# Squares of batch 0's values summed on the tensor engine, the cast of x moved to GpSimd, and a new place table

## The chip, the cores and the metric

The kernel runs on one core of a Trainium2 chip. The metric is device time in microseconds (us) of one execution: 903.31 us is the median of three runs before the change (902.73 to 905.12). The core has five engines that run side by side, each working through its own list of instructions in order: PE (matmuls), DVE (vector), ACT (activations), POOL (GpSimd) and SP, which here issues every DMA.

## The reference, cut to what matters

Attention over 4 batches, 8 heads, 768 positions and 64 dimensions. Each query and key is assigned to the nearest of 16 centroids, and a score counts only between positions of the same cluster. The result is the input of a feed-forward layer with a mish-like gate.

```python
q_assign = np.argmax(np.einsum('bhsd,hcd->bhsc', q_n, c_n), axis=-1)
k_assign = np.argmax(np.einsum('bhsd,hcd->bhsc', k_n, c_n), axis=-1)
mask = q_assign[:, :, :, None] == k_assign[:, :, None, :]
scores = np.where(mask, scale * np.matmul(q, k.transpose(0, 1, 3, 2)), -1e9)
attn = softmax(scores)
x = np.matmul(attn, v)                 # to (3072 tokens, 512)
h = x @ w_in                           # (3072, 2048)
sp = log1p(exp(h))
out = (h * np.tanh(sp)) @ w_out        # (3072, 512)
```

## The kernel before, in words

**The work.** A unit is one head of one batch and 256 query rows; there are 96 units, and each has two halves of 128 rows. For a half, PE makes a 128x768 tile of scores (`scores`, L611 and L616; the cluster mask is part of that matmul), DVE takes the row maximum (`rowmax`, L626), and ACT takes the exponential with its row sum (`expo`, L640). The two score tiles that can exist at once are the buffers of tag `S` in PSUM: a third score waits until an exponential has freed one. In the first 24 units (batch 0) the probabilities stay f32: PE transposes them (`turn`, L701), ACT copies them back (`back_t`, L717), and PE multiplies them with the raw f32 values (`pv`, L748). Later units split them into two f16 parts (L684 on ACT, L695 on DVE), which a DMA transposes, and use values that are scaled and split as well. `pv_scale` and `pv_out` put the result into a tile `xf` of 128x256; `x_out` (L817) casts it to f16 on ACT and `x_low` (L825) subtracts that on POOL to get the low part. The feed-forward part multiplies these two f16 parts with two f16 parts of the weights: `m1` (L845 to L847, three products each), mish on ACT, a high part on POOL (`e_gh`, L859) and a low part on DVE (`e_gl`, L867), and `m2` (L883 to L885).

**The scales.** The splits need a common scale for the weights and one for each batch of values. For the weights, `w_sq` lets PE multiply bf16 copies of each weight tile with themselves into a PSUM tile `gram`, whose diagonal is then the sum of squares; `w_sum` takes the diagonal and adds it up on DVE. For the values, `v_sq` (L351) squares each of a batch's four tiles on ACT and reads out a row sum; `v_sum` takes the largest of the four sums, and `v_turn`, `v_top`, `v_all` and `v_scale` spread one number over all partitions. Of batch 0 that number scales `pv_scale`'s copy of the row sums (L786).

**The head.** In the first 75 us or so all weights come in as 64-bit floats, by 32 DMAs of 512 KB, and are turned into f32 by ACT (`w_abs`, L264) and DVE (`w_f32`, L272, and `w_or`, L279). Their staging buffers are few, so a DMA can wait on SP, and hold up those behind it, until `w_or` has freed one. `warm` puts 24 groups of 8 matmuls of 128 columns on PE that only add to an unused corner of `gram` (L291).

**The order.** It is written out: `PLAN` gives each operation a place, and the program issues operations in the order of their places (`Plan.run`). An operation calls first what it depends on. So each engine's list follows from that table, and an engine that stands at an instruction whose input is late waits, with all behind it.

Of the kernel before, what the change touches and what calls it, by code (L numbers as in the profile page):

```python
# [56 lines left out]
def tile_clustered_attention_mish_ffn(  # L57
# [175 lines left out]
    wss = cp.tile([P, 32], F32, name="wss")  # L233
    nc.vector.memset(wss, 0.0)
# [58 lines left out]
    def w_sq(n):  # L293


        pl.after(("w_or", n), ("warm", 0), *((("w_sq", n - 1),) if n % 16 else ()))
        i, hf = divmod(n, 2)
        f = W[i + 1][:, hf * 512 : (hf + 1) * 512]
        if n == 16:
            pl.after(*(("warm", k) for k in range(T["warm"])))  # L300
            st["gram", 1] = ps.tile([P, 512], F32, tag="O", name=f"gram{n}", bufs=T["O"])
        o = st["gram", n // 16][:, :P]
        x = f.bitcast(BF16).rearrange("p (c n t) -> p c n t", c=4, t=2)[:, :, :, 1]
        for c in range(4):
            nc.tensor.matmul(
                o, x[:, c], x[:, c], start=(c == 0 and n % 16 == 0), stop=(c == 3 and n % 16 == 15),
                skip_group_check=True,
            )

    def w_sum(part):  # L310

        pl.after(*(("w_sq", part * 16 + n) for n in range(16)))
        n = part * 16 + 15
        junk = gp.tile([P, P], F32, tag="g", name=f"wq{n}")
        nc.vector.tensor_tensor(junk, st["gram", part][:, :P], ident, op=ALU.mult)
        nc.vector.tensor_reduce(wss[:, n : n + 1], junk, axis=AX.X, op=ALU.add)
        norm_sum(wss[:, part * 16 : part * 16 + 16], f"ws{part}", cp, f"ws{part}")
# [492 lines left out]
    def x_out(i):  # L810
# [143 lines left out]
def places(args, text):  # L954
# [4 lines left out]
    'w_load': places(spread(range(0, 32)), """  # L959
        19 25 0 32 24 26 21 89 30 83 87 91 157 189 220 251 84 86 45 43 151 132 207 305 253 293 326 329 370 371 397 428  # L960
    """),
    'centroids': places([()], """
        1
    """),
    'cent_norm': places([()], """
        2
    """),
    'cent_log': places([()], """
        3
    """),  # L970
# [3 lines left out]
    'qk_load': places(spread(range(0, 32)), """  # L974
        12 23 88 90 346 405 659 520 813 745 981 1049 1160 1273 1490 1362 1731 1732 1884 1784 2050 2087 2185 2367 2525
        2422 2597 2720 2835 2979 3008 3140
    """),
    'prep_sc': places(spread(range(0, 32)), """
        13 55 173 197 478 589 741 760 932 913 986 1251 1332 1428 1559 1431 1771 1870 2013 2066 2128 2284 2287 2479 2587
        2654 2659 2892 3005 3102 3185 3269  # L980
    """),
    'prep_hi': places(spread(range(0, 32)), """
        14 56 200 342 479 590 742 806 933 1025 1148 1252 1333 1429 1560 1662 1772 1871 2014 2067 2176 2285 2389 2480
        2588 2655 2787 2893 3006 3103 3186 3293
    """),
    'copy_t': places(spread(range(0, 32)), """
        15 58 201 364 480 593 765 823 946 1047 1149 1257 1355 1436 1582 1665 1778 1901 2041 2082 2192 2289 2429 2497
        2590 2738 2788 2896 3007 3104 3187 3296
    """),
    'w_abs': places(spread(range(0, 32)), """  # L990
        20 73 68 69 31 82 33 183 117 120 164 211 214 229 272 300 141 142 161 162 230 231 265 347 328 334 377 378 395 396
        440 477
    """),
    'cent_root': places([()], """
        22
    """),
    'cent_turn': places([()], """
        27
    """),
    'cent_put': places([()], """  # L1000
        28
    """),
    'assign_mm': places(spread((0, 1)), """
        29 54
    """),
    'prep_lo': places(spread(range(0, 32)), """
        41 57 241 373 500 591 743 839 944 1045 1154 1253 1354 1434 1581 1663 1773 1872 2015 2069 2178 2286 2411 2481
        2589 2656 2796 2894 3031 3116 3240 3294
    """),
    'copy_a': places(spread(range(0, 32)), """  # L1010
        42 59 286 415 539 618 772 930 987 1052 1155 1293 1356 1516 1583 1667 1826 1936 2042 2139 2193 2340 2448 2502
        2591 2761 2797 2945 3056 3174 3247 3344
    """),
    'v_load': places(spread(range(0, 4), range(0, 4)), """
        44 74 81 62 252 530 206 687 1109 1137 1530 1501 1907 1980 2225 2463
    """),
    'w_f32': places(spread(range(0, 32)), """
        46 98 101 104 60 108 138 194 118 121 165 238 267 266 273 301 152 148 222 280 254 262 310 365 339 343 400 408 436
        454 441 503
    """),  # L1020
    'w_or': places(spread(range(0, 32)), """
        47 99 102 105 61 109 158 257 119 122 166 239 268 270 274 327 153 149 223 281 255 271 311 366 340 344 401 409 437
        455 442 504
    """),
    'copy_z': places(spread(range(0, 32)), """
        48 77 242 374 501 592 744 840 945 1046 1176 1263 1388 1435 1604 1664 1777 1900 2048 2081 2201 2288 2412 2496
        2652 2737 2857 2895 3032 3117 3241 3295
    """),
    'assign_hot': places(spread((0, 1)), """
        49 70  # L1030
    """),
    'assign_first': places(spread((0, 1)), """
        50 71
    """),
    'assign_put': places(spread((0, 1)), """
        51 78
    """),
    'rows_z': places(spread((0, 1)), """
        52 79
    """),  # L1040
    'rows_t': places(spread((0, 1)), """
        53 80
    """),
    'hot_copy': places(spread(range(0, 32)), """
        63 187 318 473 580 594 766 842 947 1126 1177 1264 1389 1437 1605 1666 1779 1902 2072 2083 2270 2290 2430 2498
        2653 2739 2871 2897 3074 3118 3242 3297
    """),
    'copy_b': places(spread(range(0, 32)), """
        64 163 269 416 552 635 812 841 988 1048 1247 1267 1456 1526 1668 1753 1816 1932 2049 2107 2217 2300 2446 2562
        2683 2751 2858 2929 3033 3123 3249 3326  # L1050
    """),
    'scores': places(spread(range(0, 96), (0, 1)), """
# [9 lines left out]
    """),  # L1062
    'rowmax': places(spread(range(0, 96), (0, 1)), """
# [9 lines left out]
    """),  # L1073
    'expo': places(spread(range(0, 96), (0, 1)), """
# [261 lines left out]
```

## Time and profile before

| what | value |
|---|---|
| median of three runs | 903.31 us (902.73 to 905.12) |
| profiled execution | 905.48 us |
| its span, first to last instruction | 903.7 us |
| mean granted clock of PE in it | 0.985 of full speed |
| PE, ACT, DVE, POOL busy | 95%, 75%, 68%, 24% |

The profiled execution is 1.8 us longer than its span. The views show, for each engine, when it was busy and what ended each of its waits. A wait is put down to what came last. Busy PE is not always useful PE: `warm` counts as busy, and so does a matmul at half clock.

### The profile page before, as it was taken

Reading aid. Unit: us, or ns where it says so; the run is one execution under the profiler, and the core shown is the slowest. Engines: PE = TensorE matmul, PEld = TensorE weight load, DVE = VectorE, ACT = ScalarE, POOL = GpSimd, SP = SyncE. Lnnn points to the kernel's source line nnn. Section 1 sums busy time; section 2 is a strip of 40 time slices with the busy share of each in tenths; the row PEclk is TensorE's granted clock in tenths of the full one; section 3 lists DMA queues with packets and bytes.
Section 4 is the critical chain, followed back from the end, with each engine's and each line's share of the span. In section 5 each row is a group of like instructions: output and inputs, shape, how many; then the busy total and the mean of one; then the engine's idle time right before and its main releaser. Section 6 shows DMA issues by size and latency. Waiting matters only on the chain. (4 is left out here: it accounts for less than half of the span.)

```text
span 903.7 us, 16486 instructions
## 1 busy us (share of the span) xinstructions
PE 858.8 (95%) x6247; PEld 614.0 (68%) x6247; DVE 613.9 (68%) x1081; ACT 677.9 (75%) x1114; POOL 214.0 (24%) x323
## 2 busy tenths in 40 slices
PE   6788998999999999999999999999999999999997
PEld 6666776768676576586766765677666675776583
DVE  7897887887766777976866778776678766412020
ACT  4777787799899798899998988888889986421020
POOL 2110653432122322312212212132321311112020
PEclk9898999899999999999999999999999999999999
DMA  9787432275666675876957678865659667300000
GB/s 327 262 229 219 106 91 67 53 168 108 127 144 147 128 144 128 181 159 138 155 114 152 133 144 156 154 143 102 129 119 177 120 128 142 72 17 1 24 13 23
DMA packets 252398, 116.19 MB, mean 129 GB/s; under 512 B 230624, under 2 KB 232544, under 8 KB 252320
## 3 DMA queue, kind: packets, MB, share of 16 engines
q1 hardware_dynamic: 252320, 115.15, 57.6%
q8 instruction: 49, 0.80, 0.4%
q14 instruction: 29, 0.24, 0.1%
HBM read 35.68 MB, written 6.29 MB: 46 GB/s over the span
## 5 line engine op out<-in xcount | busy, mean ns | idle before, releaser
L845 PE MATMUL h<-x,w 128*128 128x256 f16 x768 | 209.9, 273 | 1.9 <-ACT u L855 1.9
L847 PE MATMUL h<-x,w 128*128 128x256 f16 x768 | 209.3, 273 | 0.0
L846 PE MATMUL h<-x,w 128*128 128x256 f16 x768 | 209.3, 273 | 0.0
L640 ACT ACTIVATE p<-s,m 128x768 f32<-128x768 f32 x192 | 172.7, 900 | 33.8 <-DVE m L626 18.9
L626 DVE TENSOR_REDUCE m<-s 128x1 f32<-128x768 f32 x192 | 180.8, 949 | 24.7 <-PE s L616 23.6
L695 DVE SCALAR_TENSOR_TENSOR hl<-p,l,hl 128x768 f16<-128x768 f32 x142 | 145.1, 1029 | 47.8 <-ACT hl L684 43.5
L883 PE MATMUL O<-w,g 128*128 128x512 f16 x384 | 146.1, 381 | 1.6 <-ACT osb L891 1.6
L884 PE MATMUL O<-w,g 128*128 128x512 f16 x384 | 145.5, 379 | 0.0
L885 PE MATMUL O<-w,g 128*128 128x512 f16 x384 | 145.5, 379 | 0.0
L684 ACT ACTIVATE hl<-p,l 128x768 f16<-128x768 f32 x142 | 130.1, 929 | 19.2 <-ACT p L640 7.7
L611 PE MATMUL s<-A,B 128*128 128x384 f32 x384 | 120.6, 396 | 24.1 <-ACT p L640 16.6
L867 DVE SCALAR_TENSOR_TENSOR g<-u,mscg,g 128x512 f16<-128x512 f32 x96 | 74.9, 793 | 98.7 <-POOL g L859 98.5
L859 POOL TENSOR_SCALAR g<-u,mscg 128x512 f16<-128x512 f32 x96 | 70.2, 736 | 221.2 <-ACT u L855 200.5
L855 ACT ACTIVATE u<-h,msch 128x512 f32<-128x512 f32 x96 | 63.7, 685 | 69.0 <-PE h L847 50.6
L616 PE MATMUL s<-Z,T 80*128 80x384 f32 x384 | 101.9, 347 | 3.1 <-DMA T<-stg 3.1
L92 ACT ACT_TABLE_LOAD x78 | 100.1, 1283 | 2.1 <-PEq L1326 0.7
L611 PEld LDWEIGHTS s<-A,B 128*128 128x128 f32 x384 | 63.3, 193 | 50.4 <-ACT p L640 30.2
L845 PEld LDWEIGHTS <-w 128*128 128x128 f16 x768 | 75.1, 98 | 21.1 <-issue 10.2
L846 PEld LDWEIGHTS <-w 128*128 128x128 f16 x768 | 75.3, 98 | 13.3 <-issue 2.5
L652 POOL TENSOR_SCALAR l<-l 128x1 f32<-128x1 f32 x90 | 28.0, 311 | 227.3 <-ACT p L640 225.5
L847 PEld LDWEIGHTS <-w 128*128 128x128 f16 x768 | 75.1, 98 | 8.7
L616 PEld LDWEIGHTS s<-Z,T 80*128 80x128 f32 x384 | 71.8, 194 | 3.7 <-DMA Z<-stg 3.4
(200 smaller groups left out, 1120.8 us busy)
## 6 DMA issues: line engine op xcount, KB each, us to landing
qk<-in_qk_dram SPq DMA_DIRECT2D x32, 384.0 KB, 4.0
stage<-in_w_in_dram SPq DMA_DIRECT2D x16, 512.0 KB, 6.9
stage<-in_w_out_dram SPq DMA_DIRECT2D x16, 512.0 KB, 6.4
vraw<-in_vP_dram SPq DMA_DIRECT2D x16, 384.0 KB, 4.4
out_dram<-osb SPq DMA_DIRECT2D x24, 256.0 KB, 2.8
A<-A SPq DMA_DIRECT2D x27, 192.0 KB, 3.2
Z<-B SPq DMA_DIRECT2D x18, 192.0 KB, 3.0
B<-T SPq DMA_DIRECT2D x18, 192.0 KB, 2.9
```

The source lines that it names most:

```text
L611: nc.tensor.matmul(s[:, j, :384], st["B", n][:, q0 : q0 + P], st["A", n][:, j * 384 : (j + 1) * 384], start=True, stop=False,)
L616: nc.tensor.matmul(s[:, j, :384], st["T", n][: D + NCL, q0 : q0 + P], st["Z", n][: D + NCL, j * 384 : (j + 1) * 384], start=False, stop=True,)
L626: nc.vector.tensor_reduce(m, st["s", i, a][:, :, :384], axis=AX.XY, op=ALU.max, negate=True)
L640: nc.scalar.activation(p.rearrange("p (n x) -> p n x", n=2), st["s", i, a][:, :, :384], AF.Exp, bias=st["m", i, a], scale=1.0, accum_out=l,)
L684: nc.scalar.activation(t[:, 0], p, AF.Copy, scale=r)
L695: nc.vector.scalar_tensor_tensor(t[:, 1], p, r, t[:, 0], op0=ALU.mult, op1=ALU.subtract)
L845: nc.tensor.matmul(o, wh, xh, start=(c == 0), stop=False)
L846: nc.tensor.matmul(o, wh, xl, start=False, stop=False)
L847: nc.tensor.matmul(o, wl, xh, start=False, stop=(c == 3))
L883: nc.tensor.matmul(o, gh, wh, start=(f == 0 and fi == 0), stop=False)
L884: nc.tensor.matmul(o, gh, wl, start=False, stop=False)
L885: nc.tensor.matmul(o, gl, wh, start=False, stop=(f == 7 and fi == 1))
```

## The change

Three things are changed. `v_sq` of batch 0 no longer squares on ACT: PE multiplies the bf16 upper half of each raw value tile with itself, six matmuls of 128 columns a tile, into a third corner of the same `gram` tile; `v_sum` of batch 0 then takes the diagonal on DVE, as `w_sum` does, through a new helper `gram_sum`. (The batch's number is thereby the largest sum over one column of the tiles, no longer the largest over one partition of one tile.) `x_out` casts on POOL. And the place table is another one throughout; the lists of all engines change, with the same instructions otherwise. `w_sum` loses two small reductions and the tile `wss`.

```diff
-    wss = cp.tile([P, 32], F32, name="wss")
-    nc.vector.memset(wss, 0.0)
...
-                o, x[:, c], x[:, c], start=(c == 0 and n % 16 == 0), stop=(c == 3 and n % 16 == 15),
+                o, x[:, c], x[:, c], start=(c == 0 and n == 16), stop=(c == 3 and n % 16 == 15),
...
+    def gram_sum(o, name, pool, tag):
+        junk = gp.tile([P, P], F32, tag="g", name=f"{name}q")
+        nc.vector.tensor_tensor(junk, o, ident, op=ALU.mult)
+        st[name] = pool.tile([P, 1], F32, tag=f"{tag}m", name=f"{name}m")
+        nc.vector.tensor_reduce(st[name], junk, axis=AX.X, op=ALU.add)
...
     def w_sum(part):
-        n = part * 16 + 15
-        junk = gp.tile([P, P], F32, tag="g", name=f"wq{n}")
-        nc.vector.tensor_tensor(junk, st["gram", part][:, :P], ident, op=ALU.mult)
-        nc.vector.tensor_reduce(wss[:, n : n + 1], junk, axis=AX.X, op=ALU.add)
-        norm_sum(wss[:, part * 16 : part * 16 + 16], f"ws{part}", cp, f"ws{part}")
+        gram_sum(st["gram", part][:, :P], f"ws{part}", cp, f"ws{part}")
...
     def v_sq(b, hp):
         pl.after(("v_load", b, hp))
+        if b == 0:
+            pl.after(("warm", 0))
+            x = vst[b, hp, "raw"].bitcast(BF16).rearrange("p (c n t) -> p c n t", c=6, t=2)[:, :, :, 1]
+            for c in range(6):
+                nc.tensor.matmul(
+                    st["gram", 0][:, 2 * P : 3 * P], x[:, c], x[:, c], start=False, stop=False, skip_group_check=True
+                )
+            return
...
     def v_sum(b):
         pl.after(*(("v_sq", b, hp) for hp in range(4)))
+        if b == 0:
+            gram_sum(st["gram", 0][:, 2 * P : 3 * P], "vs0", sm, "vs")
+            return
...
-            nc.scalar.copy(x[:, 0], st["xf", b, h // 2, qb])
+            nc.gpsimd.tensor_scalar(x[:, 0], st["xf", b, h // 2, qb], 1.0, 1.0, op0=ALU.mult, op1=ALU.mult)
...
 PLAN = {
+    'warm': places(spread(range(0, 24)), """
+        0 1 2 3 4 5 6 15 18 19 20 67 68 69 92 93 94 95 96 97 116 117 240 241
...
-    'warm': places(spread(range(0, 24)), """
-        4 5 6 7 8 9 10 11 16 17 18 34 35 36 37 38 39 40 94 95 111 112 113 133
```

On ACT, in the program's first part, this stands between the first exponential and the second (`p_0`, `p_1`: probabilities; `w`: weights; `vq`: squares; `pt`: transposed probabilities; `T`: mask rows). Before:

```order
L264 ACTIVATE w_275<-stage_293 128x512
L351 ACTIVATE vq_0_449,vm_448<-vraw_0_377 128x768
L587 ACTIVATE T_412<-oh_453,mbi,msc 16x3x128 x2
L264 ACTIVATE w_310<-stage_295 128x512
L351 ACTIVATE vq_3_468,vm_448<-vraw_3_417 128x768
L717 COPY pt_486<-q_0_0_482 128x384
L264 ACTIVATE w_567<-stage_308 128x512
L264 ACTIVATE w_567<-stage_464 128x512
L351 ACTIVATE vq_2_574,vm_448<-vraw_2_461 128x768
L351 ACTIVATE vq_1_576,vm_448<-vraw_1_446 128x768
L640 ACTIVATE p_1_595,l_0_428<-s_1_440,m_1_560 128x768
```

The same stretch of ACT in the changed kernel, from the first exponential to the fourth:

```order
L651 ACTIVATE p_0_408,l_0_409<-s_0_372,m_0_406 128x768
L262 ACTIVATE w_417<-stage_334 128x512
L728 COPY pt_430<-q_0_0_426 128x384
L598 ACTIVATE T_367<-oh_422,mbi,msc 16x3x128 x2
L262 ACTIVATE w_304<-stage_323 128x512
L651 ACTIVATE p_1_544,l_0_409<-s_1_412,m_1_443 128x768
L262 ACTIVATE w_417<-stage_347 128x512
L262 ACTIVATE w_584<-stage_433 128x512
L262 ACTIVATE w_584<-stage_502 128x512
L651 ACTIVATE p_1_588,l_0_409<-s_1_447,m_1_452 128x768
L728 COPY pt_430<-q_0_1_590 128x384
L651 ACTIVATE p_0_612,l_0_409<-s_0_562,m_0_610 128x768
```

The four squares are gone from ACT, and fewer weight tiles stand ahead of the second exponential. PE's list has at the same place, after its third score (`s_1_447`), 48 `warm` matmuls, the 24 new ones of the four value tiles, the turn of batch 0's sums (`vs0p`), 16 more `warm` ones, and then the fourth score (`s_0_562`).

On POOL, this stands around the first tiles of `x` (`qk`, `A`, `B`: query and key operands; `D`: cluster choice; `w`: weights). Before:

```order
L825 TENSOR_TENSOR x_0_0_1194<-xf_0_0_907,x_0_0_1194 128x256
L509 TENSOR_TENSOR D_1211<-D_1211,desc 128x384
L433 TENSOR_SCALAR qk_978<-qk_978,scq 128x768
L440 TENSOR_SCALAR A_1240<-qk_978 128x768
L448 TENSOR_TENSOR B_1283<-qk_978,A_1240 128x768
L330 TENSOR_SCALAR w_274<-w_275,ws0r 128x1024
L825 TENSOR_TENSOR x_0_1_1401<-xf_0_1_920,x_0_1_1401 128x256
```

And in the changed kernel:

```order
L828 TENSOR_SCALAR x_0_0_1121<-xf_0_0_939 128x256
L836 TENSOR_TENSOR x_0_0_1121<-xf_0_0_939,x_0_0_1121 128x256
L444 TENSOR_SCALAR qk_806<-qk_806,scq 128x768
L451 TENSOR_SCALAR A_1217<-qk_806 128x768
L459 TENSOR_TENSOR B_1221<-qk_806,A_1217 128x768
L520 TENSOR_TENSOR D_1241<-D_1241,desc 128x384
L828 TENSOR_SCALAR x_0_2_1361<-xf_0_2_1102 128x256
L836 TENSOR_TENSOR x_0_2_1361<-xf_0_2_1102,x_0_2_1361 128x256
L828 TENSOR_SCALAR x_0_1_1368<-xf_0_1_930 128x256
```

Each of the 48 tiles of `x` now takes two POOL instructions, mostly one behind the other, where the low part alone stood before.

## Rows read from the trace of the kernel before

**Rows 1.** The page: busy time, share of the span and instructions.

```profile
PE 858.8 (95%) x6247; PEld 614.0 (68%) x6247; DVE 613.9 (68%) x1081; ACT 677.9 (75%) x1114; POOL 214.0 (24%) x323
```

**Rows 2.** Busy time by four stretches: us, engines, granted clock, DMA share, GB/s.

```profile
0.00:72.00 72.00, 52.20 (x465) 43.50 (x466) 58.78 (x145) 46.04 (x89) 12.11 (x31) 0.89 0.83 276
72.00:200.00 128.00, 120.47 (x910) 92.07 (x909) 111.22 (x194) 104.23 (x224) 52.04 (x50) 0.95 0.42 109
200.00:780.00 580.00, 567.02 (x4065) 399.90 (x4064) 422.93 (x717) 506.60 (x770) 132.76 (x217) 1.00 0.69 137
780.00:904.00 124.00, 119.12 (x813) 78.53 (x810) 20.96 (x27) 21.06 (x33) 17.10 (x25) 1.00 0.08 22
```

**Rows 3.** PE's longest wait from 72 to 200 us: total, times, longest.

```profile
PE s L611 <- ACT p L640: 3.5, 5, 1.7
```

**Rows 4.** PE's two longest waits from 200 to 780 us.

```profile
PE s L611 <- ACT p L640: 8.4, 11, 1.8
PE h L845 <- ACT u L855: 1.6, 4, 0.8
```

**Rows 5.** ACT in order of time: start, length, instruction, idle time before it.

```profile
21.08 0.90 ACT L640 ACTIVATE p<-s,m 128x768 f32<-128x768 f32 x1
...
23.64 0.84 ACT L351 ACTIVATE vq<-vraw 128x768 bf16<-128x768 f32 x1
24.37 0.20 ACT L351 ACTIVATION_READ_ACCUMULATOR vq<-vraw 128x1 f32 x1
24.76 1.34 ACT L587 ACTIVATE T<-oh,mbi,msc 16x384 fp32r<-16x384 bf16 x2 [0.18 <-DVE Z L579]
...
27.66 0.48 ACT L717 COPY pt<-q 128x384 f32<-128x384 f32 x1
28.04 0.69 ACT L264 ACTIVATE w<-stage 128x512 f32<-128x512 f32 x1
...
32.23 0.88 ACT L640 ACTIVATE p<-s,m 128x768 f32<-128x768 f32 x1
```

**Rows 6.** PE in order of time, around its third score.

```profile
21.54 0.98 PE L611 MATMUL s<-A,B 128*128 128x384 f32 x2 [1.80 <-DVE D L549]
...
29.34 2.58 PE L291 MATMUL gram<-identb 128*128 128x128 bf16 x24
31.67 0.99 PE L611 MATMUL s<-A,B 128*128 128x384 f32 x2
...
55.00 1.32 PE L305 MATMUL gram<-w 128*128 128x128 bf16 x20
```

**Rows 7.** ACT's groups from 200 to 780 us: busy, mean ns, idle before.

```profile
L817 ACT CAST x<-xf 128x256 f16<-128x256 f32 x36 | 14.1, 395 | 2.9 <-DVE xf L808 2.8
```

**Rows 8.** Two short stretches, columns as in the second group.

```profile
70.00:77.00 7.00, 6.06 (x28) 5.18 (x29) 6.10 (x13) 4.72 (x10) 0.00 (x0) 0.53 0.96 283
158.00:166.00 8.00, 7.11 (x30) 5.88 (x30) 6.69 (x13) 5.20 (x13) 4.29 (x5) 0.58 0.28 87
```

**Rows 9.** Lines of POOL: count, ns shortest/median/longest, first and last start.

```profile
L652 POOL TENSOR_SCALAR l<-l x90: 190/190/1319, 181.5 to 773.1; 128x1 f32<-128x1 f32 x90
L859 POOL TENSOR_SCALAR g<-u,mscg x96: 687/692/1469, 196.6 to 879.1; 128x512 f16<-128x512 f32 x96
L825 POOL TENSOR_TENSOR x<-xf,x x48: 661/671/1492, 87.6 to 818.4; 128x256 f16<-128x256 f32 x48
```

**Rows 10.** All waits: POOL's for ACT's cast.

```profile
POOL x L825 <- ACT x L817: 92.5, 23, 22.5
```

**Rows 11.** DVE's two largest two-input lines: ns shortest/median/longest; then their groups' means.

```profile
L695 DVE SCALAR_TENSOR_TENSOR hl<-p,l,hl x142: 976/1017/1676, 180.5 to 787.0; 128x768 f16<-128x768 f32 x142
L867 DVE SCALAR_TENSOR_TENSOR g<-u,mscg,g x96: 709/748/1170, 198.3 to 879.8; 128x512 f16<-128x512 f32 x96
L695 DVE SCALAR_TENSOR_TENSOR hl<-p,l,hl 128x768 f16<-128x768 f32 x142 | 145.1, 1029 | 47.8 <-ACT hl L684 43.5 <-POOL hl L682 2.2 <-DMA A<-A 1.2
L867 DVE SCALAR_TENSOR_TENSOR g<-u,mscg,g 128x512 f16<-128x512 f32 x96 | 74.9, 793 | 98.7 <-POOL g L859 98.5
```

More of the change, by code (lines that the diff above doesn't have):

```diff
@@ L958 @@
 PLAN = {
-    'w_load': places(spread(range(0, 32)), """
-        19 25 0 32 24 26 21 89 30 83 87 91 157 189 220 251 84 86 45 43 151 132 207 305 253 293 326 329 370 371 397 428
+    'warm': places(spread(range(0, 24)), """
+        0 1 2 3 4 5 6 15 18 19 20 67 68 69 92 93 94 95 96 97 116 117 240 241
     """),
     'centroids': places([()], """
-        1
+        7
     """),
     'cent_norm': places([()], """
-        2
+        8
     """),
     'cent_log': places([()], """
-        3
+        9
@@ L970 @@
     """),
-    'warm': places(spread(range(0, 24)), """
-        4 5 6 7 8 9 10 11 16 17 18 34 35 36 37 38 39 40 94 95 111 112 113 133
+    'cent_root': places([()], """
+        10
+    """),
+    'cent_turn': places([()], """
+        11
+    """),
+    'cent_put': places([()], """
+        12
     """),
     'qk_load': places(spread(range(0, 32)), """
-        12 23 88 90 346 405 659 520 813 745 981 1049 1160 1273 1490 1362 1731 1732 1884 1784 2050 2087 2185 2367 2525
-        2422 2597 2720 2835 2979 3008 3140
+        13 29 124 102 242 400 614 531 798 714 926 1116 1148 1276 1500 1360 1723 1727 1867 1792 2024 2090 2190 2314 2487
+        2426 2576 2716 2881 2963 3005 3131
@@ L984 @@
-        2588 2655 2787 2893 3006 3103 3186 3293
+        17 57 194 342 455 603 676 819 900 1028 1131 1247 1336 1437 1575 1655 1775 1869 2016 2067 2177 2273 2376 2492
+        2570 2670 2784 2878 3021 3090 3185 3276
+    """),
+    'w_load': places(spread(range(0, 32)), """
+        22 21 26 37 28 40 31 134 44 51 112 135 132 173 161 235 80 98 47 36 146 175 238 298 234 255 299 319 330 340 387
+        420
+    """),
+    'w_abs': places(spread(range(0, 32)), """
+        23 25 27 62 30 99 41 166 74 119 144 216 176 217 219 272 125 126 159 160 182 237 305 327 316 317 359 360 410 411
+        439 472
@@ L985 @@
+    """),
+    'w_f32': places(spread(range(0, 32)), """
+        24 81 65 88 48 100 72 178 108 120 163 232 230 254 253 293 147 127 226 294 208 257 306 350 334 336 395 375 461
+        418 440 473
+    """),
+    'v_load': places(spread(range(0, 4), range(0, 4)), """
+        45 32 34 35 225 452 156 655 1084 1157 1546 1502 1900 1981 2332 2365
     """),
     'copy_t': places(spread(range(0, 32)), """
-        15 58 201 364 480 593 765 823 946 1047 1149 1257 1355 1436 1582 1665 1778 1901 2041 2082 2192 2289 2429 2497
@@ L988 @@
[L988 to L1004, printed above, removed]
+        33 59 195 358 456 632 741 822 973 1045 1132 1260 1337 1438 1576 1656 1776 1883 2017 2070 2197 2276 2441 2512
@@ L1012 @@
-        2591 2761 2797 2945 3056 3174 3247 3344
+        39 60 271 437 567 636 779 887 1025 1064 1159 1283 1370 1501 1585 1722 1848 1948 2061 2110 2198 2284 2442 2565
+        2601 2743 2836 2977 3077 3155 3250 3375
     """),
-    'v_load': places(spread(range(0, 4), range(0, 4)), """
-        44 74 81 62 252 530 206 687 1109 1137 1530 1501 1907 1980 2225 2463
+    'assign_hot': places(spread((0, 1)), """
+        42 66
     """),
-    'w_f32': places(spread(range(0, 32)), """
-        46 98 101 104 60 108 138 194 118 121 165 238 267 266 273 301 152 148 222 280 254 262 310 365 339 343 400 408 436
-        454 441 503
+    'assign_first': places(spread((0, 1)), """
+        43 75
@@ L1050 @@
-        2683 2751 2858 2929 3033 3123 3249 3326
+        63 162 279 436 546 649 780 823 974 1047 1229 1321 1456 1517 1664 1743 1812 1936 2055 2094 2209 2327 2476 2529
+        2659 2751 2862 2929 3034 3122 3262 3301
     """),
     'scores': places(spread(range(0, 96), (0, 1)), """
[9 rows of a table removed]
[9 rows of a table added]
     """),
     'rowmax': places(spread(range(0, 96), (0, 1)), """
[9 rows of a table removed]
[9 rows of a table added]
     """),
     'expo': places(spread(range(0, 96), (0, 1)), """
[9 rows of a table removed]
[9 rows of a table added]
+    """),
+    'turn': places(spread(range(0, 24), (0, 1), (0, 1)), """
[4 rows of a table added]
+    """),
@@ new lines @@
+    'back_t': places(spread(range(0, 24), (0, 1), (0, 1)), """
[4 rows of a table added]
+    """),
+    'v_sq': places(spread(range(0, 4), range(0, 4)), """
+        103 104 105 106 528 896 613 811 1123 1237 1603 1696 1937 2095 2353 2555
+    """),
+    'v_sum': places(spread(range(0, 4)), """
+        107 897 1717 2556
+    """),
+    'v_turn': places(spread(range(0, 4)), """
+        110 954 1718 2557
+    """),
+    'v_top': places(spread(range(0, 4)), """
+        111 955 1719 2558
+    """),
+    'p_hi': places(spread(range(0, 96), (0, 1)), """
[9 rows of a table added]
@@ new lines @@
+    """),
+    'v_all': places(spread(range(0, 4)), """
+        122 967 1725 2632
+    """),
+    'v_scale': places(spread(range(0, 4)), """
+        123 968 1726 2633
+    """),
+    'w_sq': places(spread(range(0, 32)), """
+        138 139 140 141 154 155 259 282 283 284 285 287 289 290 291 345 377 378 379 380 381 382 383 392 393 394 479 480
+        502 503 519 582
+    """),
+    'pair_mm': places(spread(range(2, 31, 2)), """
+        157 453 665 902 1117 1308 1559 1757 1918 2152 2373 2551 2758 2979 3168
@@ L1125 @@
+    """),
+    'invert': places(spread(range(0, 96), (0, 1)), """
[9 rows of a table added]
+    """),
+    'pair_hot': places(spread(range(2, 31, 2)), """
+        177 469 673 903 1121 1324 1560 1758 1919 2153 2374 2552 2766 2985 3175
+    """),
+    'ptrans': places(spread(range(0, 96), (0, 1)), """
[9 rows of a table added]
     """),
     'p_lo': places(spread(range(0, 96), (0, 1)), """
[9 rows of a table removed]
[9 rows of a table added]
     """),
-    'v_sum': places(spread(range(0, 4)), """
-        125 902 1721 2534
+    'invert_pair': places(spread(range(0, 12)), """
+        203 339 427 547 611 605 744 842 915 990 1052 1119
@@ L1151 @@
     """),
     'v_split': places(spread(range(0, 4), range(0, 4)), """
-        139 198 354 150 973 976 1043 1050 1819 1894 1854 1851 2748 2623 2753 2824
+        370 368 467 239 1002 1015 1034 1067 1834 1894 1876 1855 2695 2651 2869 2760
+    """),
+    'pair_put': places(spread(range(2, 31, 2)), """
+        261 539 740 978 1172 1348 1599 1781 2048 2235 2421 2603 2863 3029 3226
+    """),
+    'pv_scale': places(spread(range(0, 96)), """
[5 rows of a table added]
+    """),
+    'pv_out': places(spread(range(0, 96)), """
[5 rows of a table added]
@@ L1154 @@
+    """),
+    'x_out': places(spread(range(0, 96)), """
[5 rows of a table added]
+    """),
+    'x_low': places(spread(range(0, 96)), """
[5 rows of a table added]
+    """),
+    'w_sum': places(spread((0, 1)), """
+        363 583
     """),
     'v_low': places(spread(range(0, 4), range(0, 4)), """
-        140 199 355 407 974 1003 1044 1083 1833 1895 1885 1852 2749 2647 2874 2964
-    """),
-    'invert': places(spread(range(0, 96), (0, 1)), """
[9 rows of a table removed]
-    """),
-    'pair_mm': places(spread(range(2, 31, 2)), """
-        172 467 669 903 1122 1304 1554 1750 1923 2152 2368 2552 2766 2980 3166
```

118 lines of the change are left out of this document (35 added, 83 removed), and 280 rows, old and new, of the table PLAN.

## The prediction

> **What bounds the kernel now.** I read the page's busy shares first. PE is busy 858.8 of 903.7 us, and no other engine is above 75% [rows 1]. So the time is PE's work plus what PE stands idle, and a change that leaves PE's work as it is can win only idle time, or time at half clock.
>
> The table by stretches then shows where that idle time lies [rows 2]. In the first 72 us PE idles 72 - 52.2 = 19.8 us; from 72 to 200 us 128 - 120.5 = 7.5; from 200 to 780 us 580 - 567.0 = 13.0; after 780 us 4.9, which is mostly the last result's way out. In the first 72 us DVE is the busiest engine (58.8), and ACT, with 46.0, stands still for want of data; from 200 to 780 us ACT is the busiest after PE (506.6 of 580).
>
> PE's waits say for whom. From 72 to 200 us the largest is for the exponential on ACT, 3.5 us [rows 3]; from 200 to 780 us ACT ends 8.4 + 1.6 = 10.0 of the 13.0 us [rows 4]. No wait of PE for POOL is among these. Last I looked at the granted clock: it is below full in the first 72 us (0.89) and in two short stretches later, 0.53 over 7 us and 0.58 over 8 us, with PE busy nearly throughout [rows 2, 8]. Between the two levels, 1.2 and 2.4 GHz, that costs about 0.47 x 7 = 3.3 and 0.42 x 8 = 3.4 us. Each follows waits of PE.
>
> **The squares off ACT (first 72 us).** Before, the second exponential starts 32.23 - 21.08 = 11.2 us after the first [rows 5]. Four squares stand between them, each 0.84 us and 0.2 us of read-out, so 4.1 us. The changed list has five instructions there: two weight tiles of 0.69, one copy of 0.48 and two mask rows of 1.34 together, 3.2 us in all [rows 5]. The second exponential could so start 7 to 8 us earlier, which frees the score buffer for PE's third score (31.67 before, after the second at 21.54 [rows 6]). I don't take 7 us for it. DVE is busy 58.8 of these 72 us and has the same work ahead of the later row maxima in either list, so what a lead can win is at most DVE's 13.2 free us, part of which is the start; and the weights still have to come in over DMA queues that are 83% busy [rows 2]. On the other side the new list puts 48 and 16 `warm` matmuls and the 24 new ones ahead of the fourth score. I take -3.0 us, less than half of the lead; bounds are -8.0 (all of it stays) and +3.0 (late values or weights put the stalls elsewhere).
>
> **The squares on PE.** 24 matmuls of 128 columns: 20 of that form took 1.32 us at full clock, 24 took 2.58 us where the clock was low [rows 6], so 1.6 to 2.6 us. They stand where PE idles 19.8 us in all, so idle time covers most of it. DVE's diagonal comes on top of the way to batch 0's number, but that number is wanted only by `pv_scale`, after the first units' `pv`. +0.5 us; without the cover it is 2.6. The two small reductions that go, and the memset, are covered by other DVE work: nothing, bounds -0.5 and +0.5.
>
> **The cast off ACT.** From 200 to 780 us 36 casts hold ACT 14.1 us and a further 2.9 idle in front of it for `xf` [rows 7], 17.0 us. ACT's free time there is 580 - 506.6 = 73.4 us and becomes 90.4 [rows 2]. If PE's waits for ACT shrink in that ratio, 10.0 us become 8.1: -1.9 us. At the ends, none of the waits shrinks, or all 10.0 go. From 72 to 200 us there are at most the other 12 casts, 4.7 us beside 23.8 free ones: 3.5 x 4.7 / 28.5 = -0.6 us, with ends at 0 and -3.5. The table loads on ACT are the same number in both lists.
>
> **The cast on POOL.** No row has this form. The nearest are one column at 190 ns, 512 columns at 692 ns, and the two-input form with the same 256 columns at 671 ns [rows 9]. The line through the first two gives 0.44 us at 256, and I take that: 48 x 0.44 = 21 us, between 48 x 0.19 = 9 and 48 x 0.67 = 32. POOL has room, being busy 24% [rows 1]. It also waited 92.5 us for ACT's cast before its own low part [rows 10], and that hop between engines is gone, so the low part should come no later than before. What the new POOL work can cost is DVE's: of DVE's two-input instructions a few were far longer than the rest, 1676 against a median of 1017 ns, and 1170 against 748. But the means are only 1029 and 793 ns, so all of it came to 142 x 0.012 + 96 x 0.045 = 6.0 us [rows 11], in a kernel whose POOL was busy 214 us. A tenth more POOL work makes that some 0.6 us more. +0.5, bounds -2 (`x` comes earlier) and +8 (below).
>
> The Trainium skill (SBUF — State Buffer, Who interferes with whom) says that GpSimd shares a pair of SBUF ports with VectorE, that a VectorE instruction with two SBUF inputs contends with a GpSimd one that reads SBUF, and that the loser waits for the other's whole instruction. That speaks against moving the cast. By it each cast that meets such a DVE instruction would cost DVE or POOL up to its length; the trace shows long instances, but their sum is 6.0 us and not a multiple [rows 11]. By the trace the term stays at +0.5; by the rule at its hardest the last rival below is what comes.
>
> **The new table.** It moves everything, and each stall of PE is thrown anew. The order of attention and feed-forward work on PE after 200 us is nearly the same in both lists, so I take 0, and let the range hold +4 and -4 for it.
>
> **Sum.** -3.0 + 0.5 - 1.9 - 0.6 + 0.5 = -4.5 us. Against the profiled execution that is 905.48 - 4.5 = 901.0; that execution was 2.2 us over the median of the runs, so against the median it is 903.31 - 4.5 = 898.8 us.
>
> **Rivals.**
> *The lead stays whole.* PE's third and later scores come 7 us or so earlier, PE does not stand before the stretch at 70 to 77 us, and its clock stays full there: -8.0 - 3.3 - 1.9 - 0.6 + 0.5 + 0.5 = -12.8, or 890.5 us. For it speaks that ACT, DVE and PE all had waits in the first 40 us [rows 5, 6]; against it that DVE has little room there.
> *The lead is given back.* DVE's list and the arrival of weights set the pace to 75 us, or PE stands at the new matmuls for the value tile that SP loads last (behind a weight tile that waits for its staging buffer). Then the first term is 0, and new stalls eat the small ones: 901 to 905, about 903 us. That the change does nothing for the time is this case.
> *POOL holds up DVE.* The place is every cast of `x` that meets a two-input or copying instruction on DVE, in front of which row maxima queue up. The price is 0.44 us each: 12 casts outside the middle, where DVE has 16.8 free us from 72 to 200, give 5.3; of the 36 others PE feels a fifth, 3.2. With the lead lost too, 0 + 0.5 - 2.5 + 8.5 = +6.5, so 910 us. It makes the kernel slower from the point where the casts hold PE up by more than the 4.5 + 0.5 us won elsewhere, 60% of that price. Against it speaks that POOL's 48 low parts, of the same size and longer, leave no wait of PE behind them.
>
> **How the numbers follow.** A measurement of this kernel tells a change from none at about 0.3%, 2.7 us: below 900.6 is faster, above 906.0 slower. Forecast 0.50, its own range 893 to 903, so 0.40 faster and 0.10 same. The whole lead 0.14, faster. The lead given back 0.22, of it 0.18 same and 0.04 slower. POOL holding DVE 0.14, slower. Together 0.54, 0.28 and 0.18. The range that leaves out 2 in 10 is 889 to 908.
>
> **What would show it.** The second exponential starts within 5 us of the first, and PE idles about 17 us up to 72 us instead of 19.8; if the idle time there is unchanged, the first term was wrong. PE's waits for ACT from 200 to 780 us fall from 10.0 to about 8, and ACT's busy time falls by about 23 us (48 casts of 0.395 and 4.1 for the squares). The cast on POOL has a median near 0.44 us, and the means of DVE's two-input lines [rows 11] rise by under 20 ns; if they rise by 100 ns or more, the last rival is there. The forecast is wrong as a whole if PE's idle time after 200 us changes by more than 4 us, since then the new table, not the moved work, set the time.

## The result and the profile after

The changed kernel takes 888.5 us (median of 4 runs, 887.8 to 888.8) against 903.9 us before (902.7 to 905.1): a ratio of 0.983, 95% interval 0.981 to 0.985. The forecast was 898.8 us with a range from 889 to 908; the gain is 15.4 us where 4.5 were forecast. The profiled execution after took 888.56 us, its span is 886.7 us: 17.0 us less than the span of before.

The first part of the page after, busy time and share of the span, answers to [rows 1]:

```profile
PE 852.1 (96%) x6271; PEld 609.7 (69%) x6271; DVE 613.2 (69%) x1079; ACT 659.8 (74%) x1058; POOL 235.8 (27%) x371
```

PE is busy 6.7 us less than in [rows 1], though it has 24 matmuls more, and idles 886.7 - 852.1 = 34.6 us where it was 44.9. These two numbers are the 17.0 us of the spans. Where they lie is seen in the stretches of [rows 2], and behind them the two short ones of [rows 8], columns as there:

```profile
0.00:72.00 72.00, 58.87 (x566) 49.78 (x567) 65.32 (x156) 49.42 (x95) 12.16 (x32) 0.93 0.86 297
72.00:200.00 128.00, 119.90 (x930) 90.29 (x929) 111.75 (x190) 105.57 (x213) 56.73 (x66) 1.00 0.44 107
200.00:780.00 580.00, 571.52 (x4126) 405.69 (x4124) 422.40 (x717) 489.88 (x729) 155.18 (x257) 1.00 0.72 137
...
70.00:77.00 7.00, 5.41 (x40) 4.26 (x37) 5.83 (x11) 4.42 (x10) 1.57 (x2) 1.00 0.93 272
158.00:166.00 8.00, 7.44 (x53) 5.47 (x54) 7.41 (x12) 6.67 (x14) 4.37 (x6) 1.00 0.15 31
```

PE's idle time is now 13.1 us to 72 us (before 19.8), 8.1 to 200 us (7.5) and 8.5 to 780 us (13.0). In the two short stretches the granted clock is full, where it was 0.53 and 0.58. PE gets more done there, though it is not the same work: from 158 to 166 us it has 53 recorded matmuls instead of 30. PE's busy time fell because less of it ran at half clock (1.2 instead of 2.4 GHz). By the granted clock of the stretches, 0.11 x 72 + 0.05 x 128 = 14.3 us up to 200 us were lost to it in [rows 2], and 0.07 x 72 = 5.0 us are lost now. So about half of the 17.0 us is clock, and the rest is idle time.

The next lines are PE's longest waits after, from 72 to 200 us (the first) and from 200 to 780 us, as in [rows 3, 4]:

```profile
PE s L622 <- ACT p L651: 4.5, 7, 1.6
...
PE s L622 <- ACT p L651: 4.2, 7, 1.2
PE h L856 <- ACT u L866: 3.1, 3, 1.6
```

From 200 to 780 us PE waits 7.3 us for ACT instead of 10.0. Now PE in order of time around its third score, as in [rows 6], and under it ACT's first two exponentials, as in [rows 5]:

```profile
19.78 0.98 PE L622 MATMUL s<-A,B 128*128 128x384 f32 x2
...
22.73 0.99 PE L622 MATMUL s<-A,B 128*128 128x384 f32 x2
...
24.16 3.43 PE L289 MATMUL gram<-identb 128*128 128x128 bf16 x48
27.43 1.54 PE L352 MATMUL gram<-vraw 128*128 128x128 bf16 x24
30.03 0.27 PE L208 MATMUL vs0p<-ident,vs0m 128*1 128x128 f32 x1 [1.07 <-DVE vs0m L312]
30.14 1.05 PE L289 MATMUL gram<-identb 128*128 128x128 bf16 x16
31.01 0.60 PE L622 MATMUL s<-A,B 128*128 128x384 f32 x2
...
20.54 0.90 ACT L651 ACTIVATE p<-s,m 128x768 f32<-128x768 f32 x1 [0.41 <-DVE m L637]
...
27.39 0.90 ACT L651 ACTIVATE p<-s,m 128x768 f32<-128x768 f32 x1
```

The third score comes at 22.73 us instead of 31.67, the fourth at 31.01 instead of 35.02. The second exponential stands 6.9 us behind the first instead of 11.2. PE's lead, by which I mean how much earlier the score of the same number starts, is 8.9 us at the third score, 4.0 at the fourth, 2.5 at the 7th (41.0 us; before 43.5), 9.3 at the 9th (47.5; 56.8), 8.4 at the 17th (75.4; 83.8), 8.3 at the 33rd (117.8; 126.1), 11.6 at the 53rd (171.1; 182.7), behind the second half-clock stretch, 17.1 at the 97th (357.5; 374.6) and 17.4 at the last (753.4; 770.8). So most of what the early third score won is gone by the 7th, and the lead that stays is made behind it. (PE does other work between the scores in another order, so single steps of the lead say little.)

The cast on POOL, its duration in ns shortest/median/longest as in [rows 9], then the groups of POOL's two lines on `x` and of DVE's two lines of [rows 11], with mean ns:

```profile
L828 POOL TENSOR_SCALAR x<-xf x48: 400/407/1232, 71.5 to 777.9; 128x256 f16<-128x256 f32 x48
...
L828 POOL TENSOR_SCALAR x<-xf 128x256 f16<-128x256 f32 x48 | 27.2, 569 | 59.6 <-DVE xf L819 34.5 <-DVE xf L816 24.0
L836 POOL TENSOR_TENSOR x<-xf,x 128x256 f16<-128x256 f32 x48 | 36.3, 759 | 3.2
L706 DVE SCALAR_TENSOR_TENSOR hl<-p,l,hl 128x768 f16<-128x768 f32 x142 | 147.2, 1042 | 61.6 <-ACT hl L695 58.3 <-POOL hl L693 1.5 <-DMA qk<-in_qk_dram 0.7
L878 DVE SCALAR_TENSOR_TENSOR g<-u,mscg,g 128x512 f16<-128x512 f32 x96 | 73.5, 777 | 87.9 <-POOL g L870 87.6
```

A cast's median is 407 ns, but its mean 569: POOL is the one held up, and it has the time. DVE's two lines went from 1029 to 1042 and from 793 to 777 ns. The low part no longer waits 92.5 us for ACT [rows 10]; it stands right behind its cast.

### The profile page after: what moved, and what is told of

Same layout as the page of the kernel before. It is cut to its first block, busy times and chain, and to the rows that moved or that the text cites. A ratio compares the mean times of both kernels' runs of the same rounds, so it can differ in the third digit from the quotient of the medians.

```text
span 886.7 us, 16505 instructions
## 1 busy us (share of the span) xinstructions
PE 852.1 (96%) x6271; PEld 609.7 (69%) x6271; DVE 613.2 (69%) x1079; ACT 659.8 (74%) x1058; POOL 235.8 (27%) x371
## 5 line engine op out<-in xcount | busy, mean ns | idle before, releaser
L706 DVE SCALAR_TENSOR_TENSOR hl<-p,l,hl 128x768 f16<-128x768 f32 x142 | 147.2, 1042 | 61.6 <-ACT hl L695 58.3
L622 PE MATMUL s<-A,B 128*128 128x384 f32 x384 | 118.8, 390 | 15.5 <-ACT p L651 11.5
L663 POOL TENSOR_SCALAR l<-l 128x1 f32<-128x1 f32 x90 | 25.7, 285 | 233.4 <-ACT p L651 231.6
```

The lines of the kernel that those rows point to most:

```text
L622: nc.tensor.matmul(s[:, j, :384], st["B", n][:, q0 : q0 + P], st["A", n][:, j * 384 : (j + 1) * 384], start=True, stop=False,)
L706: nc.vector.scalar_tensor_tensor(t[:, 1], p, r, t[:, 0], op0=ALU.mult, op1=ALU.subtract)
```

## The experiments

The theory after the result: the new order of the head gave the gain, not the moved work. Its rivals: the squares off ACT, the cast off ACT, or both together gave it; or the half-clock stretches did. Each kernel was timed against the kernel before on the same chip, whose medians there were 903.9 to 905.5 us. All compute the whole result.

**The moved work without the new table.** Three kernels keep the old place table: the squares moved (the six-matmul loop and `gram_sum`), the cast moved, both. The edits are those lines of the change alone:

```diff
-            nc.scalar.copy(x[:, 0], st["xf", b, h // 2, qb])
+            nc.gpsimd.tensor_scalar(x[:, 0], st["xf", b, h // 2, qb], 1.0, 1.0, op0=ALU.mult, op1=ALU.mult)
```

Squares alone: 

> The old place table with batch 0's squares on PE, the cast still on ACT. Theory A (the moved work made the gain): the four squares (4.1 us) leave ACT between the first two exponentials, so the second starts 4 to 8 us earlier than 32.2 and the time falls by 4 to 8 us. Theory B (the new table made it): with the old order DVE still does eight weight instructions before the second row maximum, and the time falls by less than 2 us.

Measured 905.0 us, ratio 1.000 (0.998 to 1.002).

Cast alone: 

> The old place table with the cast of x on POOL, squares on ACT. Theory A: 48 casts of 0.39 us leave ACT, PE's waits for ACT from 200 to 780 us fall by a third or more, time down 3 to 5 us. Theory B: down 0 to 2 us. The theory that POOL holds up DVE: up by 2 us or more.

Measured 905.0 us, ratio 1.001 (0.999 to 1.003).

Both: 

> Both pieces of moved work with the old table. Theory A: most of the 15 us, so 889 to 893 us. Theory B: 899 to 902 us.

Measured 906.6 us, ratio 1.002 (1.000 to 1.004). In the old order the moved work wins nothing. Why the squares don't is seen in the kernel with the squares alone. Its DVE line of the second row maximum, and then ACT's second exponential:

```profile
29.77 0.96 DVE L637 TENSOR_REDUCE m<-s 128x1 f32<-128x768 f32 x1
...
31.13 0.88 ACT L651 ACTIVATE p<-s,m 128x768 f32<-128x768 f32 x1
```

The second exponential still stands 10.0 us behind the first (21.09), though no square is there: the row maximum it needs is done only at 30.73, and PE's third score, at 31.35, is only 0.3 us earlier than in [rows 6]. The same in the trace of before, first the second row maximum on DVE, then PE, columns as in [rows 5]:

```profile
29.07 0.96 DVE L626 TENSOR_REDUCE m<-s 128x1 f32<-128x768 f32 x1
...
26.97 0.40 PE L305 MATMUL gram<-w 128*128 128x128 bf16 x4 [0.48 <-DVE w L279]
28.03 0.63 PE L305 MATMUL gram<-w 128*128 128x128 bf16 x8 [0.66 <-DVE w L279]
29.09 0.40 PE L305 MATMUL gram<-w 128*128 128x128 bf16 x4 [0.43 <-DVE w L279]
```

The second score ended at 23.2 us, yet its row maximum starts at 29.07: on DVE's list four pairs of weight instructions stand ahead of it. PE's third score, for which the first exponential had left a buffer free at 22 us, stands on PE's list behind 24 matmuls of `w_sq`, which wait for the same weight tiles, and behind 24 of `warm`. So the two lists held both, and the squares on ACT lay beside them. In the changed kernel DVE has the row maximum further ahead:

```profile
25.30 0.96 DVE L637 TENSOR_REDUCE m<-s 128x1 f32<-128x768 f32 x1
```

and PE's third score follows the second with only mask and transpose matmuls between.

**The new table without one of the moves.** First the new table with the squares left on ACT:

```diff
-        if b == 0:
-            pl.after(("warm", 0))
-            x = vst[b, hp, "raw"].bitcast(BF16)...
-            for c in range(6):
...
```

> The new table and the cast on POOL, but batch 0's squares back on ACT, at the places that the new table gives them (they stand together before the second turn of batch 0's sums). Theory A: 4 to 8 us slower than the changed kernel, 893 to 897 us, with the half-clock stretches back. Theory B: within 2 us of it, 887 to 891 us.

Measured 889.7 us (888.2 to 890.2), ratio 0.983 (0.980 to 0.986): nearly the whole gain. Its third and fourth score on PE, and ACT's second exponential:

```profile
22.01 0.60 PE L611 MATMUL s<-A,B 128*128 128x384 f32 x2
...
32.90 0.99 PE L611 MATMUL s<-A,B 128*128 128x384 f32 x2
...
30.75 0.90 ACT L640 ACTIVATE p<-s,m 128x768 f32<-128x768 f32 x1
```

Here the four squares do hold up the second exponential (10.6 us behind the first, at 20.18) and the fourth score (32.90 instead of 31.01), and it costs 1 us or so in the end. The squares are worth that: 889.7 - 888.5 = 1.2 us, about what the runs scatter.

Then the new table with the cast on ACT. Three of the 48 casts had to be placed earlier, since on ACT they would stand behind an instruction that waits for their own buffer:

```diff
+EARLIER = {(16,): 1004.5, (29,): 1496.5, (70,): 2848.5}
+PLAN['x_out'] = [(args, EARLIER.get(args, place)) for args, place in PLAN['x_out']]
+PLAN['x_low'] = [(args, EARLIER.get(args, place - 0.25) + 0.25) for args, place in PLAN['x_low']]
```

Neither move: 

> The new table alone: squares and cast both on ACT (three casts and low parts of x are placed a little earlier, since on ACT they may not stand behind the next tile's first writer). Theory B: 888 to 892 us. Theory C (the new table is worth its time only because ACT is freed of the casts, 18.8 us): 895 us or more, with PE's waits for ACT from 200 to 780 us back at 10 us or above.

Measured 918.7 us, ratio 1.015 (1.013 to 1.017): slower than before.

Squares moved, cast on ACT: 

> The new table with the squares on PE, the cast on ACT (with the same three tiles of x placed earlier). Theory B: 888 to 892 us. Theory C: 893 us or more, and the loss arises after 200 us, since only 10 of the 48 casts lie before.

Measured 919.3 us, ratio 1.016 (1.014 to 1.019).

The changed kernel with those three casts moved, as a control: 

> A control: the changed kernel with the three tiles of x placed earlier as in the two runs with the cast on ACT, the cast left on POOL. If those runs lost their 30 us to the cast's place on ACT: within 2 us of the changed kernel, 887 to 891 us. If the three moved tiles did the harm: 895 us or more.

Measured 887.3 us (887.0 to 889.5), ratio 0.982 (0.980 to 0.984). So the three places cost nothing, and the cast is worth 919.3 - 887.3 = 32 us in the new order (31 if each kernel is held against the kernel before on its own chip) and none in the old. The table needs the cast on POOL; the two can't be priced apart.

**Where the table wins.** One order up to a place, the other behind it, both moves made (the rule by which the table is put together):

```python
place = {o: new[o] if new[o] < cut else 10000 + old[o] for o in new}
```

The head new, place 1170 being about 170 us: 

> Both pieces of moved work; the order of the new table up to its place 1170 (about where the first feed-forward tile starts, 180 us), and behind that the rest in the old table's order. Theory B1 (the order of the head alone made the gain, and the later order only carries it): the lead of 11 to 12 us at 200 us stays, 891 to 894 us. Theory B2 (the order behind the head adds as much on its own): half of the gain, 895 to 899 us.

Measured 892.8 us against 905.4, ratio 0.987 (0.984 to 0.989).

The head old, new behind 1170: 

> The reverse: the old table's order up to its place 1170, then the new table's. B1: 899 to 902 us, the 3 to 5 us that the changed kernel wins after 200 us. B2: 893 to 897 us. If the two halves only fit together (neither order does alone), both hybrids are at 900 us or above.

Measured 901.5 us, ratio 0.996 (0.994 to 0.998). The two parts, 12.6 and 3.9 us, add up to 16.5, about the whole.

New only to place 180, about 40 us: 

> Both pieces of moved work, the new table's order up to its place 180 (about the first 40 us), then the old table's. B3: the lead of the head arises there, 893 to 897 us. B4: 898 to 903 us.

Measured 900.4 us (898.3 to 907.2), ratio 0.997 (0.993 to 1.000). The third score is at 22.7 us, but only 4 to 5 us of lead are left at 200 us.

New to place 560, about 75 us: 

> Both moves, the new order for places up to 560 (about the first 75 us), the old order behind it. New order to place 180 gave 900.4 us, to place 1170 892.8. If the head's part of the gain is the lead of the first 75 us, 893 to 894; if it is made between 75 us and the half-clock stretch at 159 us, 898 to 901 and that stretch is there again.

Measured 900.0 us, ratio 0.995 (0.993 to 0.997), the second outcome. Two waits of PE in this kernel, and the stretch behind them; columns as in [rows 6] and [rows 2]:

```profile
149.82 0.62 PE L622 MATMUL s<-A,B 128*128 128x384 f32 x2 [1.74 <-ACT p L651]
152.58 0.37 PE L208 MATMUL vs1p<-ident,vs1m 128*1 128x128 f32 x1 [0.87 <-DVE xf L816]
...
151.00:162.00 11.00, 10.13 (x46) 7.54 (x46) 9.59 (x19) 7.09 (x14) 7.99 (x8) 0.53 0.19 63
```

The kernel with the new order to place 1170, same views:

```profile
148.28 0.27 PE L208 MATMUL vs1p<-ident,vs1m 128*1 128x128 f32 x1 [0.54 <-DVE xf L816]
148.64 0.59 PE L622 MATMUL s<-A,B 128*128 128x384 f32 x2
...
151.00:162.00 11.00, 10.43 (x80) 7.37 (x79) 10.30 (x17) 10.04 (x21) 5.02 (x7) 1.00 0.12 28
```

With the cut at 560 PE stands 1.74 us at its 44th score and 0.87 at the turn of batch 1's sums (`vs1p`), and half clock follows, as in the kernel before:

```profile
156.91 0.62 PE L611 MATMUL s<-A,B 128*128 128x384 f32 x2 [1.74 <-ACT p L640]
159.43 0.37 PE L208 MATMUL vs1p<-ident,vs1m 128*1 128x128 f32 x1 [0.89 <-DVE xf L805]
```

With the new order the turn stands ahead of the 44th score and waits 0.54 us (a transpose just before it 0.82), that score waits for nothing, the clock stays full, and PE does 80 instead of 46 matmul records in 11 us. Of the 7.2 us between these two kernels 0.47 x 11 = 5.2 are that stretch.

**One cause taken alone, in the old order.** The second row maximum, exponential and third score moved to early places:

```diff
+MOVED = {('rowmax', (0, 1)): 79.5, ('expo', (0, 1)): 80.5, ('scores', (1, 0)): 93.5}
+PLAN = {name: [(args, MOVED.get((name, args), place)) for args, place in rows] for name, rows in PLAN.items()}
```

> The kernel before with three places changed: the second row maximum and the second exponential go ahead of the weight instructions and squares that stood in front of them on DVE and ACT, and the third score ahead of the matmuls of the weights' squares. Theory B3 (the head's lead comes from the second exponential no longer standing behind weights and squares): the third score starts near 28 us instead of 31.7, and 4 to 8 us of lead stay at 72 us: 896 to 900 us. Theory B4 (the lead comes from the order of loads and weights over the whole head): back to the old times by the tenth score, 902 to 906 us.

Measured 906.4 us, ratio 1.003 (1.001 to 1.004). The third score comes at 23.9 us, and PE then stands for what is behind it:

```profile
23.85 0.99 PE L611 MATMUL s<-A,B 128*128 128x384 f32 x2
...
34.36 0.27 PE L208 MATMUL vs0p<-ident,vs0m 128*1 128x128 f32 x1 [2.48 <-DVE vs0m L201]
...
36.43 0.99 PE L611 MATMUL s<-A,B 128*128 128x384 f32 x2
```

The fourth score is later than before (36.43 against 35.02). One early step is not the lead. That the steps behind it have to be early too fits this, but no run takes them one by one.

Filler matmuls on PE ahead of the waits before both half-clock stretches, into an unused corner:

```diff
+    def fill(part, count):
...
+PLAN['fill'] = [((0, 40), 352.5), ((1, 24), 939.5), ((1, 12), 963.5)]
```

> The kernel before with matmuls of 128 columns that fill three waits of PE: 40 ahead of the score that waits 3.1 us for a DMA at 70.9 us, 24 ahead of the score that waits 1.7 us at 156.9 us, 12 ahead of the turn at 159.4 us; their sums go to an unused corner of gram. If the half-clock stretches at 70 to 77 and 158 to 166 us follow from these waits: both gone and 4 to 7 us won, 897 to 900 us. If not: 903 to 907 us.

Measured 907.1 us (903.8 to 910.1), ratio 1.002 (1.001 to 1.004). The two stretches of [rows 8] in its profiled execution, which took 903.8 us:

```profile
70.00:77.00 7.00, 7.00 (x83) 6.41 (x81) 6.18 (x13) 4.95 (x12) 0.00 (x0) 1.00 1.01 300
158.00:166.00 8.00, 7.01 (x54) 4.84 (x53) 6.70 (x15) 5.43 (x13) 5.83 (x5) 1.00 0.26 82
```

The clock is full in both in this execution. In the second PE still stands 1.0 us, but no longer more than 0.40 us at once, so the stretches do hang on the long waits. The time was not better, though. The ten runs go from 903.8 us at a mean granted clock of 0.992 to 910.1 at 0.985, and at one clock the filled kernel is the slower one: at 0.988 it took 904.6 to 907.4 us, the kernel before 903.2 to 904.5. So the filling costs some 1 to 4 us elsewhere, and by the mean clock the gain in clock does not come in each run. That the two stretches are worth 6.7 us by themselves is not shown.

**Why the new order needs the cast off ACT.** In the kernel at 919.3 us this is one of the stalls, engine by engine (POOL, DVE, ACT, PE), and the stretch behind it:

```profile
238.48 0.67 POOL L836 TENSOR_TENSOR x<-xf,x 128x256 f16<-128x256 f32 x1 [6.59 <-ACT x L828]
239.21 0.19 POOL L663 TENSOR_SCALAR l<-l 128x1 f32<-128x1 f32 x1
...
239.44 0.16 DVE L675 RECIPROCAL l<-l 128x1 f32<-128x1 f32 x1 [3.17 <-POOL l L663]
239.52 1.02 DVE L706 SCALAR_TENSOR_TENSOR hl<-p,l,hl 128x768 f16<-128x768 f32 x1
...
240.57 0.90 ACT L651 ACTIVATE p<-s,m 128x768 f32<-128x768 f32 x1 [2.17 <-DVE hl L706]
244.18 0.90 ACT L651 ACTIVATE p<-s,m 128x768 f32<-128x768 f32 x1 [0.57 <-DVE hl L706]
...
245.23 0.62 PE L622 MATMUL s<-A,B 128*128 128x384 f32 x2 [1.86 <-ACT p L651]
...
246.00:253.00 7.00, 5.64 (x29) 3.90 (x28) 4.17 (x8) 6.89 (x9) 1.77 (x3) 0.51 0.85 143
```

POOL stands 6.59 us at the low part for ACT's cast; behind it waits the small product of the row sums, for that DVE, for that ACT's next exponential. PE's next wait is for the exponential after that one, and half clock follows. Between 200 and 780 us there are five such half-clock stretches, 24 us in all, and the changed kernel has none. PE's idle time there is 580 - 557.2 = 22.8 us, against 580 - 571.3 = 8.7 in the control. So in this stretch about 12 us are lost to the clock and 14 to waits. POOL's standing alone is no loss: in the kernel before it stands 56.2 us for the cast from 200 to 780 us, and nothing was won by taking that away. Two things can lie behind the loss: ACT's load, or this hop, by which I mean POOL standing for a result of ACT with other work queued behind it. First the load alone, without a wait:

```diff
             nc.gpsimd.tensor_scalar(x[:, 0], st["xf", b, h // 2, qb], 1.0, 1.0, op0=ALU.mult, op1=ALU.mult)
+            for _ in range(2):
+                nc.scalar.copy(aside, ident[:, :64])
```

> The changed kernel, cast on POOL as it is (with the three tiles moved as in the control), and in addition two copies of 128x64 f32 to f16 of a constant on ACT at each of the 48 casts, which nothing waits for and which wait for nothing. It puts back on ACT about the cast's load (0.395 us each, 18.8 us in all), without its waits. Theory A, the 30 us lost with the cast on ACT come from ACT's load behind which exponentials and mish stand: about 905 to 919 us, PE's waits for the exponential from 200 to 780 us 8 us or more. Theory B, they come from ACT standing still for xf and from the hop from ACT to POOL: 887 to 891 us, those waits 4 to 5 us.

Measured 896.5 us (895.5 to 899.1), ratio 0.990 (0.988 to 0.993): neither theory's number. ACT was busy 677.8 us, as in [rows 1]. The load costs 896.5 - 887.3 = 9.2 us. PE's two waits for ACT from 200 to 780 us are 12.2 us where they are 7.5 in the control, and the clock is full there.

Then the cast on ACT, with the low part placed later on POOL, so that POOL stands less for it:

```diff
+LATER = {(3,): 427, (4,): 557, (5,): 548, ...}
+PLAN['x_low'] = [(args, LATER.get(args, place)) for args, place in PLAN['x_low']]
```

> The kernel with the new table, squares on PE and the cast on ACT (919.3 us), but x_low stands up to 24 places (some 6 us) later on POOL, where no first writer of a later xf and no m1 stands between; 33 of the 48 are moved by 8 places or more. ACT's load and its waits for xf stay; what goes is POOL standing at x_low for ACT's cast, with the small instruction on the row sums (128x1) behind it for which DVE waits. In the trace at 919 us POOL stood 87.6 us for the cast from 200 to 780 us. Theory A, the hop from ACT to POOL costs the 22 us that the load alone doesn't explain: 896 to 905 us, POOL's wait for the cast at most half of 87.6 us, and the half-clock stretches behind 200 us mostly gone. Theory B, ACT standing still for xf, or its load at just those places, costs them: 914 to 922 us.

Measured 907.4 us (903.6 to 909.0), ratio 1.002 (1.000 to 1.004), again between the two. POOL's wait for the cast and PE's two longest waits from 200 to 780 us; first the kernel at 919.3 us:

```profile
POOL x L836 <- ACT x L828: 87.6, 23, 9.3
...
PE s L622 <- ACT p L651: 12.5, 10, 3.1
PE h L856 <- ACT u L866: 5.7, 5, 1.9
```

and with the low part later:

```profile
POOL x L836 <- ACT x L828: 28.4, 10, 5.3
...
PE s L622 <- ACT p L651: 9.4, 10, 2.7
PE h L856 <- ACT u L866: 5.6, 7, 1.9
```

Two thirds of POOL's standing are gone and 12 us with them; of the five half-clock stretches two are left, 7 us instead of 24, so most of the 12 us is clock. So of the 32 us 9.2 go with ACT's load and 12.0 with POOL's standing, if the two add up, which no run tests. The other 10.8 are open: a part of the hop is still there (28.4 us), and ACT's standing for `xf` was not taken away by itself.

## Why the prediction was wrong, by its steps

**"The new table ... so I take 0."** This is the step that failed. With both moves and the old table the time is 906.6 us, with the new one 888.5. The step argued from PE's order after 200 us, which is nearly the same. But the orders of DVE and ACT in the head are not, and there, up to about 170 us, the new order won 12.6 us; behind it, where the argument was made, 3.9, just inside the bound of 4. The prediction's own sign for this case (PE's idle time after 200 us changes by more than 4 us) came: 13.0 to 8.5.

**The squares off ACT, -3.0.** Squares alone: 0.0 (0.998 to 1.002), in the new order some 1 us. The reading of the stretch between the first and the second exponential was wrong: it counted what stood on ACT, and not what the second exponential waited for. Its row maximum stood on DVE's list until 29.07 us and was done at 30.03, so four squares less could win at most 32.23 - 30.03 = 2.2 us of the 7 to 8. PE's third score was put down to the exponential's buffer; it stood behind `w_sq` on PE. The idle time to 72 us fell by 6.7 instead of 3, but not by that cause.

**The cast off ACT, -1.9 and -0.6.** In the old order nothing was won (1.001), and PE's two waits for ACT from 200 to 780 us were 9.6 us with both moves, where the ratio of free times had asked for 8.1. In the new order the same move decides over 32 us. That a wait shrinks as the other engine's free time grows was the failed assumption: a wait hangs on the one instruction that is late. The forecast never asked what the new order would do with the cast where it was.

**The squares on PE, +0.5, and the cast on POOL, +0.5.** Right: the 24 matmuls took 1.54 us, between the third and the fourth score, where PE has only `warm` besides, a cast 407 ns (0.44 taken), and DVE's lines changed by +13 and -16 ns, under the 20 that were named. The sum of the casts was 27.2 us and not 21: 12 of the 48 took 0.83 us or more, and each of these overlaps a two-input instruction of DVE in the trace; POOL had room for it. By the Trainium skill's rule (SBUF — State Buffer, Who interferes with whom), weighed in the prediction, one of two such instructions waits for the other's whole length. The trace agrees in kind: long casts are there, to 1232 ns. But the one held up was mostly POOL, and the rival that builds on the rule did not come.

**The clock.** Two half-clock stretches were read and priced, 3.3 and 3.4 us, but left out of the sum; both went. Only the rival of the whole lead took in the first. That rival, 890.5 us at a chance of 0.14, is the nearest to what came (888.5), but by luck. It took 8.0 us of lead and 3.3 of clock, 11.3 by the end of the first stretch; measured are 8.4 at the 17th score, which starts behind that stretch. It left out the second stretch and took 0 for the table, and the cause that it names, the squares, was not the cause.

**Three signs that were named.** ACT's busy time fell by 18.1 us, not 23. The second exponential is 6.9 us behind the first, not within 5, and the kernel with the squares on ACT shows that this distance says little: there it is 10.6 and the time 889.7 us.

## What to carry to other kernels

Where a change moves a little work and orders everything anew, price the order first: for each engine in the stretch with the most idle time, look at what the late instruction waits for in the old list, and what stands ahead of that in the new one. An operation's place and its engine belong together: the same cast was worth nothing in one order and 32 us in the other, of which 12 went with what was queued behind the instruction that waited for it. And a short wait of PE is worth more than its length where half clock follows it; so count such stretches into the sum when their waits move, though filling two such waits alone won nothing here.

## What the runs showed of the hardware

- Half clock followed waits of PE that were short: 1.74 and 0.87 us gave about 10 us at half clock (0.53 from 151 to 162 us, the order cut at 560), 1.86 and 1.36 us (at 245 and 247 us, the kernel at 919.3 us) gave about 7. But a single wait of 1.59 us, at 75.4 us in the changed kernel, was followed by full clock.
- The new order with the cast on POOL scattered less: 887.0 to 890.2 us over three kernels with 4 runs each, where the kernel before and the three with its table ran from 901 to 910 us, in more runs. It is not the order alone: with the cast on ACT and the low part later, the new order ran from 903.6 to 909.0. In the kernel before the scatter goes with the mean granted clock: it took 902.2 to 903.5 us in seven runs at 0.986 to 0.990, 908.3 to 909.3 in three at 0.979 to 0.981. What makes the same program get another clock was not tried.
- The cast of 128x256 f32 to f16 takes 407 ns on POOL and 395 on ACT [rows 7]. Where POOL's cast met a two-input instruction of DVE, it took up to 1232 ns, which adds 7.8 us over 48 casts, and DVE's means hardly moved.
